# A new order of VectorE and ScalarE work between two layers, and block products of 384 + 384 columns

## The chip, the cores and the metric

The kernel runs on one core of a Trainium2 chip. The metric is the device time of one execution in microseconds. Three runs of the kernel before took 812.77 to 813.53 us, median 813.25. One more execution was taken by the profiler. PE is TensorE (PEld its weight loads), DVE is VectorE, ACT is ScalarE, POOL is GpSimd, SP issues most DMAs.

## The reference

```python
mask = q_assign[:, :, :, None] == k_assign[:, :, None, :]     # nearest of 16 centroids
scores = np.where(mask, scale * np.matmul(q, k.transpose(0, 1, 3, 2)), -1e9)
attn_out = softmax(scores) @ v            # 2 x 8 heads, 768 tokens, 64 channels
x = attn_out.transpose(0, 2, 1, 3).reshape(1536, 512)
h = x @ w_in                              # layer 1, 512 -> 2048
x = softplus(h) @ w_out                   # 2048 -> 512
g = x @ w_gate                            # layer 2, 512 -> 1536
y = (g * sigmoid(g) * (x @ w_val)) @ w_out2   # 1536 -> 512
```

The attention's inputs are float32, the weights float64 in this case, the result float32. Every matmul outside the transposes is made of three: each operand is split into a high part in the engine's rounded float32 form and the low remainder, and high x high, high x low and low x high are summed in PSUM.

## The kernel before

The attention fills the first 250 us or so; the change does not touch it. After it the 1536 tokens lie as columns of `XH` and `XL` (high and low part), with the 512 channels in four pieces of 128 rows.

**Layer 1** runs over 16 *units* of 128 hidden columns (`h_unit`). A unit multiplies the four channel pieces of its weight with all tokens into three PSUM banks of 512 columns (36 matmuls, `proj`). ACT then reads each bank twice (Abs into `e`, Relu into `r`), takes Exp and Ln of `e`, DVE adds `r` and `e`, ACT casts the sum to its high part `gh`, and DVE subtracts for the low part `gl`. Two units at a time go into `y_group(g)`, which multiplies with their `w_out` rows. It has four *blocks*, one for each 128 output channels, of three banks and 18 matmuls: nine for the first unit, nine for the second. DVE adds each bank to `acc`. There are eight banks, handed out in turn, so that a block's third bank can be the one that a unit or block some banks earlier still holds. On PE, units 14 and 15 stand before y_group 6 (units 12 and 13) and y_group 7 (units 14 and 15). In y_group 7 the finished `acc` is also split into `YH` (ACT) and `YL` (DVE and POOL), the input of layer 2.

**Weights** come as 512 KB loads (`raw`, three buffers). Each float64 weight is narrowed to float32: ACT takes the Abs of the upper words, DVE does two TENSOR_SCALAR and two SCALAR_TENSOR_TENSOR (`m`), then the split into `whi` (a cast, by DVE in layer 1, by ACT in layer 2) and `wlo` (DVE). This work is cut into three tasks per weight (`first`, `second`, `third`) in a deque `todo`; `pump` takes a few tasks from it after each piece of matmuls. So the order in which the program text calls tasks is the order of each engine's queue, and every engine works its queue strictly from the front.

**Layer 2** has 12 units. The first two are *plain*: gate and val products of 36 matmuls each (`plain_unit`), Silu of the gate banks on ACT into `sg`, product with the val banks on DVE. The other ten (`s_unit`) use a block scheme with seven products of half the inner size and half the tokens instead of eight. For it `t_sums` makes four differences of quarters of `acc` (in place, DVE) and splits each into `Th` (ACT) and `Tl` (DVE). One product (`prod`) has 2 x 3 weights and for each weight two matmuls, of 512 and of 256 columns, into a tile of 768 of two banks. The results go through tiles `x`, `w`, `y`, ACT copies and DVE additions. The second matrix `w_out2` is applied in `o_piece`, 12 matmuls for 256 tokens into a tile of two banks, one for each 128 tokens (a *token tile*); nine such pieces at the end are added to the earlier result by DVE, one addition per token tile, and stored.

The lines that matter: L858, L859 (`split_g`), L877 to L888 (`h_unit`), L908 to L930 (`y_group`), L1032 to L1045 (`t_sums`), L1072 and L1081 (`plain_unit`), L1096 (`o_piece`), L1124 (`prod`), L1156 (first copy of an `s_unit`), L1225 and L1229 (the last additions), L123 to L150 (narrowing and splitting a weight).

Of the kernel before, what the change touches and what calls it, by code (L numbers as in the profile page):

```python
# [11 lines left out]
F32 = mybir.dt.float32  # L12
# [3 lines left out]
AF = mybir.ActivationFunctionType  # L16
# [24 lines left out]
def kernel(  # L41
# [143 lines left out]
    def pair_of(f):  # L185
        return [(("gate", f), cols_of(w_gate, f), None), (("val", f), cols_of(w_val, f), None)]
# [4 lines left out]
    for f in range(NF2):  # L191
        stream += (pair_of(f + 1) if NPLAIN <= f + 1 < NF2 else []) + last_of(NF1 + f)
# [40 lines left out]


# [631 lines left out]
    def h_unit(f, banks=None):  # L866
        if banks is None:
            banks = [bank() for _ in range(NCH)]
            w = need(W, ("in", f))
            for half in range(2):  # L870
                proj(XH, XL, w, banks, range(2 * half, 2 * half + 2))
                pump()
        e = tp.tile([128, NTOK], F32, tag="e", name="e")
        r = tp.tile([128, NTOK], F32, tag="s", name="r")
        for c in range(NCH):
            cs = slice(512 * c, 512 * c + 512)
            nc.scalar.activation(out=e[:, cs], in_=banks[c], func=AF.Abs)  # L877
# [12 lines left out]
        def split_part():  # L890
            g_t[f] = split_g(e, "g")

        return [log_part, sum_part, split_part], split_tasks(batches.pop(0))

    def y_group(g):
# [3 lines left out]
        for d0 in range(0, KD, nd):  # L899
# [31 lines left out]
            if not last:  # L931
                pump()

# [4 lines left out]
    for g in range(NF1 // 2):  # L938
        if 2 * g + 2 < NF1:
            for f in (2 * g + 2, 2 * g + 3):  # L940
                soft, split = h_unit(f)
                if f < NF1 - 2:
                    todo.extend([soft[0]] + split[:3] + [soft[1]] + split[3:6] + [soft[2]] + split[6:])
                else:
                    first_do(soft + split[:3])
                    todo.extend(split[3:])
        else:
            YH = keep.tile([128, KD, NTOK], F32R, tag="xh", name="YH")
            YL = keep.tile([128, KD, NTOK], F32R, tag="xl", name="YL")
# [31 lines left out]
    S_t, T_t = {}, {}  # L981
# [47 lines left out]
    def t_sums():  # L1029

        q = [[acc[:, 2 * k:2 * k + 2, HT * t:HT * t + HT] for t in range(2)] for k in range(2)]
        nc.vector.tensor_tensor(out=q[0][0], in0=q[0][1], in1=q[0][0], op=ALU.subtract)  # L1032
        nc.vector.tensor_tensor(out=q[0][1], in0=q[1][1], in1=q[0][1], op=ALU.subtract)
        nc.vector.tensor_tensor(out=q[1][1], in0=q[1][1], in1=q[0][0], op=ALU.subtract)
        nc.vector.tensor_tensor(out=q[1][0], in0=q[1][0], in1=q[1][1], op=ALU.subtract)

# [10 lines left out]
        tasks = []  # L1047
        for n, x in ((3, q[0][1]), (2, q[1][1]), (4, q[1][0]), (1, q[0][0])):
            tasks += [functools.partial(high, n, x), functools.partial(low, n, x)]
        return tasks  # L1050

    def plain_unit(f):
        gb = [bank() for _ in range(NCH)]
        wg = need(W, ("gate", f))
        if f == 0:
            vb = [bank() for _ in range(NCH)]
            wv = need(W, ("val", f))
            proj(YH, YL, wg, gb, range(KD - 1))
            pump2(4)
            proj(YH, YL, wv, vb, range(KD - 1))  # L1060
            pump2(3)
            proj(YH, YL, wg, gb, range(KD - 1, KD))
            proj(YH, YL, wv, vb, range(KD - 1, KD))
            pump2(2)
# [50 lines left out]
    def s_unit(f):  # L1115
# [59 lines left out]
        y = psx.tile([128, 1024], F32, tag="Y", name="y")[:, 0:HT]  # L1175
# [11 lines left out]
        a_half(f, sg, 0)  # L1187
        a_half(f, sg, 1)
# [3 lines left out]
    todo.extend(split_tasks(last_of(NF1)))  # L1192
    todo.extend(plain_unit(0))
    todo.extend(pair_tasks(2))
    todo.extend(split_tasks(last_of(NF1 + 1)))
# [66 lines left out]
```

## Time and profile before

| what | us |
| --- | --- |
| median of three runs | 813.25 |
| the profiled execution | 813.9 |
| its span, first to last instruction | 812.1 |
| PE busy in the span | 791.0 |
| DVE busy | 654.5 |
| ACT busy | 500.8 |

The time of an execution is 1.8 us more than its span. Start times below count from the span's beginning. A matmul's row shows its start and a modelled duration that overlaps with the next one, so the pace of PE is read from the distance between starts. A bracket at a row's end says how long the engine sat idle before it and which instruction ended that.

### The profile page before, as it was taken

What the parts mean: (1) busy time and instruction counts of PE and PEld (TensorE: products, weight loads), DVE (VectorE), ACT (ScalarE), POOL (GpSimd) and SP (SyncE); (2) the same over time, 40 slices, a digit from 0 to 9 for tenths busy, and PEclk for the clock granted to TensorE, in tenths of its full rate; (3) what the DMA queues carried; (4) which work ended last, traced back from release to release, by engine and by line L of the source; (5) the groups of instructions that cost most, each with busy time, mean ns of one, the idle gap of its engine ahead of it and who ended that gap; (6) DMA issues with size and microseconds to landing.
All of it is one profiled execution on the core that took longest, in us unless ns stands there. A gap on an engine that the chain in (4) does not pass through costs nothing.

```text
span 812.1 us, 12093 instructions
## 1 busy us (share of the span) xinstructions
PE 791.0 (97%) x4485; PEld 689.6 (85%) x4485; DVE 654.5 (81%) x1047; ACT 500.8 (62%) x893; POOL 163.0 (20%) x160
## 2 busy tenths in 40 slices
PE   8999999999999999999999999989999999999997
PEld 7898999999998778888888887867888888888886
DVE  6988988888895997989879778889777777777763
ACT  5888889889895587365563744355544655555520
POOL 5736456555522000000000000400000101011100
PEclk9999999999999999999999999999999999999999
DMA  7875865675411322222121210012435676767454
GB/s 177 238 180 128 204 145 145 168 164 138 98 40 31 104 78 78 76 81 78 52 78 55 76 52 28 25 39 92 155 132 115 144 147 138 154 120 142 85 176 155
DMA packets 69339, 91.57 MB, mean 113 GB/s; under 512 B 29376, under 2 KB 52000, under 8 KB 69280
## 3 DMA queue, kind: packets, MB, share of 16 engines
q1 hardware_dynamic: 64688, 79.40, 34.6%
q0 software_dynamic: 3024, 11.01, 9.0%
q8 instruction: 35, 0.57, 0.3%
q10 hardware_dynamic: 1568, 0.39, 0.2%
q14 instruction: 24, 0.20, 0.1%
HBM read 51.41 MB, written 17.35 MB: 85 GB/s over the span
## 4 chain that ended last, share of the span: by engine, by line
PE 81%; DVE 12%; ACT 3%; DMA 2%; issue 1%; POOL 0%; DVEq 0%; ACTq 0%; SPq 0%; POOLq 0%
PE bank L908 14%; PE bank L818 13%; PE ob L1096 12%; PE x L1124 10%; PE ops L558 7%; PE tps L541 7%; PE sps L509 7%; PE w L1124 5%; PE y L1124 3%; PE mps L383 1%; PE sims L420 1%; DVE m L135 1%; DVE m L132 1%; DVE acc L922 1%; DVE wlo L150 1%
## 5 line engine op out<-in xcount | busy, mean ns | idle before, releaser
L548 DVE TENSOR_TENSOR tl<-tps,th 128x384 fp32r<-128x384 f32 x192 | 98.8, 550 | 14.8 <-ACT th L547 14.5
L517 DVE TENSOR_REDUCE nm<-sps 128x1 f32<-128x768 f32 x96 | 91.3, 952 | 14.1 <-PE sps L509 11.5
L547 ACT CAST th<-tps 128x384 fp32r<-128x384 f32 x192 | 84.6, 490 | 18.6 <-PE tps L541 16.0
L541 PE MATMUL tps<-id,p 128*128 128x128 f32 x576 | 93.1, 278 | 1.5 <-DVE tl L548 1.5
L525 ACT ACTIVATE p<-sps,nm 128x768 f32<-128x768 f32 x96 | 88.2, 919 | 1.6 <-DVE nm L517 1.6
L509 PE MATMUL sps<-KT,QT 128*128 128x384 f32 x384 | 83.4, 339 | 1.7 <-ACT p L525 1.7
L541 PEld LDWEIGHTS tps<-id,p 128*128 128x128 f32 x576 | 75.1, 151 | 8.1 <-DVE tl L548 4.2
L558 PE MATMUL ops<-th,VV 128*128 128x256 f32 x288 | 80.1, 307 | 0.0
L558 PE MATMUL ops<-tl,VV 128*128 128x256 f32 x288 | 72.7, 282 | 0.0
L858 ACT CAST gh<-e 128x1536 fp32r<-128x1536 f32 x16 | 23.8, 1487 | 73.0 <-DVE e L888 73.0
L509 PEld LDWEIGHTS sps<-KT,QT 128*128 128x128 f32 x384 | 63.3, 189 | 2.6 <-ACT p L525 2.4
L1113 POOL DMA_DIRECT2D out_dram<-side x21 | 18.2, 868 | 227.5 <-ACT side L1109 227.5
L150 DVE TENSOR_TENSOR wlo<-m,whi 128x512 fp32r<-128x512 f32 (+1 forms) x66 | 43.0, 651 | 24.2 <-ACT whi L149 22.5
L930 POOL TENSOR_TENSOR YL<-acc,YH 128x512 fp32r<-128x512 f32 x7 | 9.3, 1322 | 260.6 <-ACT YH L924 260.4
L922 DVE TENSOR_TENSOR acc<-bank,acc 128x512 f32<-128x512 f32 x84 | 53.0, 681 | 6.4 <-PE bank L908 6.4
L908 PE MATMUL bank<-gh,whi 128*128 128x512 f32 x192 | 54.5, 391 | 2.2 <-DVE whi L149 1.1
L1096 PE MATMUL ob<-whi,aa 128*128 128x512 f32 x168 | 56.5, 390 | 0.0
L558 PEld LDWEIGHTS ops<-tl,VV 128*128 128x128 f32 x288 | 54.7, 190 | 0.1
L818 PE MATMUL bank<-XH,whi 128*128 128x512 f32 x192 | 54.1, 390 | 0.7 <-DVE whi L149 0.7
L558 PEld LDWEIGHTS ops<-th,VV 128*128 128x128 f32 x288 | 54.4, 189 | 0.2
L908 PE MATMUL bank<-gl,whi 128*128 128x512 f32 x192 | 54.0, 389 | 0.0
L908 PE MATMUL bank<-gh,wlo 128*128 128x512 f32 x192 | 54.0, 389 | 0.0
(199 smaller groups left out, 1938.4 us busy)
## 6 DMA issues: line engine op xcount, KB each, us to landing
raw<-in_moe_w_out_dram SPq DMA_DIRECT2D x28, 512.0 KB, 3.3
out_dram<-side POOLq DMA_DIRECT2D x21, 512.0 KB, 5.6
raw<-in_moe_w_in_dram SPq DMA_DIRECT2D x16, 512.0 KB, 3.7
raw<-in_moe_w_val_dram SPq DMA_DIRECT2D x12, 512.0 KB, 4.4
raw<-in_moe_w_gate_dram SPq DMA_DIRECT2D x12, 512.0 KB, 3.4
QT<-hi SPq DMA_DIRECT2D x30, 192.0 KB, 3.0
KT<-hi SPq DMA_DIRECT2D x14, 384.0 KB, 5.6
kn<-in_k_dram SPq DMA_DIRECT2D x16, 192.0 KB, 3.9
```

The source lines that it names most:

```text
L509: nc.tensor.matmul(ps[:, c, 0:384], lhsT=Q[:, a, 128 * j:128 * j + 128], rhs=K[:, a, 384 * c:384 * c + 384], start=(a == 0), stop=(a == 1),)
L517: nc.vector.tensor_reduce(out=nm, in_=ps[:, :, 0:384], axis=AX.XY, op=ALU.max, negate=True)
L525: nc.scalar.activation(out=_h(p), in_=s_t.pop(i)[:, :, 0:384], func=AF.Exp, bias=nm_t.pop(i), accum_out=sm_t[pr][:, j:j + 1],)
L541: nc.tensor.transpose(ps[:, 128 * j:128 * j + 128], p[:, 128 * kb:128 * kb + 128], id32)
L547: nc.scalar.copy(th, pv)
L548: nc.vector.tensor_tensor(out=tl, in0=pv, in1=_r(th), op=ALU.subtract)
L558: nc.tensor.matmul(o[:, 0:CW], lhsT=VV_t[pr][:, hh, kb].rearrange("p a d -> p (a d)"), rhs=t[:, kb, :], start=(kb == 0 and lohi == 0), sto ...
L818: nc.tensor.matmul(banks[c], lhsT=wt[:, kk, :], rhs=xt[:, kk, 512 * c:512 * c + 512], start=(kk == 0 and wt is hi and xt is xh), stop=(kk ...
L908: nc.tensor.matmul(banks[NCH * d + c], lhsT=wt[:, 0, ds_], rhs=gt[:, 512 * c:512 * c + 512], start=(ff == 0 and n == 0), stop=(ff == 1 and ...
L922: nc.vector.tensor_tensor(out=a, in0=bk, in1=a, op=ALU.add)
L1096: nc.tensor.matmul(bk[:, t, :], lhsT=lhs[:, ts_], rhs=rhs[:, 0, :], start=(ff == 0 and i == 0), stop=(ff == 1 and i == 2),)
L1124: nc.tensor.matmul(dst[:, cs], lhsT=wt[:, at + kk, :], rhs=x(part, kk)[:, cs], start=(first and kk == 0 and wt is hi and part == 0), stop= ...
```

## The change

- Units 14 and 15: the weight rows 14 and the gate weight 1 are now narrowed between the steps of unit 14's softplus, and rows 15 inside y_group 6. `h_unit(15)` and the blocks of y_groups 6 and 7 take given numbers of tasks instead of what `pump` chooses.
- Both `w_out2` weights of the plain units are loaded earlier and narrowed in y_group 7 (`two_tasks`), with the cast on ACT; `high_on` is set before y_group 7.
- The first T difference is made inside y_group 7; the other three and three of the four `Th` casts follow in one task, the last `Th` comes after the first plain unit's Silu.
- A one-column Silu of the identity, with a one-column DVE copy behind it, stands ahead of the first real Silu, so that the table is loaded there.
- `prod` uses 384 + 384 columns, each half in a bank of its own; `sg`, `p1`, `x`, `w`, `y` are viewed accordingly.
- `o_piece` finishes one token tile before it begins the other.

```diff
+    def two_tasks(keys, tag):
+        m_t = {}
+        def first():
+            for key in keys:
+                while key not in loaded_t:
+                    load_ahead(len(loaded_t) + 1)
+                m_t[key] = w_narrow(loaded_t.pop(key))
+                next(m_t[key])
...
+        return [first, second, third] + [functools.partial(split, key) for key in keys]
...
                 proj(XH, XL, w, banks, range(2 * half, 2 * half + 2))
-                pump()
+                if f < NF1 - 1:
+                    pump()
+                else:
+                    for _ in range(4):
+                        todo.popleft()()
...
+    def t_sum(n):
+        nc.vector.tensor_tensor(
+            out=quad[(0, 0, 1, 1)[n]][(0, 1, 1, 0)[n]],
+            in0=quad[(0, 1, 1, 1)[n]][(1, 1, 1, 0)[n]],
+            in1=quad[(0, 0, 0, 1)[n]][(0, 1, 0, 1)[n]],
+            op=ALU.subtract,
+        )
...
-            if not last:
+            if g == NF1 // 2 - 2:
+                for _ in range((0, 2, 1, 9)[d0]):
+                    if todo:
+                        todo.popleft()()
+            elif not last:
                 pump()
+            elif d0 < 3:
+                for _ in range((2, 1, 2)[d0]):
+                    late.popleft()()
+                if d0 == 1:
+                    t_sum(0)
...
-                    first_do(soft + split[:3])
-                    todo.extend(split[3:])
+                    while todo and todo[0] in begun:
+                        todo.popleft()()
+                    todo.extendleft(reversed([soft[0]] + split[:3] + [soft[1]] + split[3:5] + [soft[2]] + split[5:]))
...
+            high_on.append(1)
+            while todo:
+                todo.popleft()()
+            late = collections.deque(two_tasks([("out2", f) for f in range(NPLAIN)], "b"))
         y_group(g)
...
+        def sums():
+            for n in range(1, 4):
+                t_sum(n)
+            for n, x in order[:3]:
+                high(n, x)
...
+        if f == 0:
+            nc.scalar.activation(out=sg[:, 0:1], in_=id32[:, 0:1], func=AF.Silu)
+            nc.vector.tensor_copy(sg[:, 0:1], id32[:, 0:1])
...
-        for ff in range(2):
-            hi, lo = need(W, ("out2", 2 * g + ff))
-            ah, al = (x[n // 3] for x in a_t[2 * g + ff])
-            for t in range(2):
+        for t in range(2):
+            for ff in range(2):
+                hi, lo = need(W, ("out2", 2 * g + ff))
+                ah, al = (x[n // 3] for x in a_t[2 * g + ff])
...
-                    for cs in CH:
+                    for c in range(2):
                         nc.tensor.matmul(
-                            dst[:, cs],
+                            dst[:, c, :],
                             lhsT=wt[:, at + kk, :],
-                            rhs=x(part, kk)[:, cs],
+                            rhs=x(part, kk)[:, HT // 2 * c:HT // 2 * c + HT // 2],
```

First place: ACT's queue after unit 14. `e_5695` and `gh_5745` or `gh_5761` belong to unit 14, `raw_5543` is weight rows 14, `raw_5667` rows 15, `raw_5609` gate weight 1, `bank_5703` to `bank_5705` the banks of unit 15. In the kernel before:

```order
L885 ACTIVATE e_5695<-e_5695 128x1536 [waits Activation_49]
L858 CAST gh_5745<-e_5695 128x1536 [waits DVE_49]
L123 ACTIVATE m_5749<-raw_5543 128x512 [waits DMAHW0_49]
L877 ACTIVATE e_5753<-bank_5703 128x512 [waits PE_49]
L881 ACTIVATE r_5754<-bank_5703 128x512
```

And in the changed kernel:

```order
L916 ACTIVATE e_5695<-e_5695 128x1536 [waits Activation_49]
L123 ACTIVATE m_5726<-raw_5543 128x512 [waits DMAHW0_49]
L123 ACTIVATE m_5757<-raw_5609 128x512 [waits DMAHW1_49,DVE_49]
L885 CAST gh_5761<-e_5695 128x1536 [waits DVE_49]
L908 ACTIVATE e_5765<-bank_5703 128x512 [waits PE_49]
```

The Abs of two weights now stand ahead of unit 14's cast; the reads of unit 15's banks stand behind that cast in both.

Second place: DVE's queue from unit 14's addition (`e_5695`) to the first `acc` additions of y_group 6. `m_5749` and `m_5726` are weight rows 14, `m_5757` gate weight 1, `m_5783` rows 15, `bank_5761` and `bank_5787` the first bank of y_group 6. In the kernel before:

```order
L888 TENSOR_TENSOR e_5695<-r_5696,e_5695 128x1536 [waits Activation_49]
L859 TENSOR_TENSOR gl_5746<-e_5695,gh_5745 128x1536 [waits Activation_49]
L125 TENSOR_SCALAR m_5749<-m_5749 128x512 [waits Activation_49]
L128 TENSOR_SCALAR m_5749<-m_5749 128x512 [waits DVE_49]
L922 TENSOR_TENSOR acc_4053<-bank_5761,acc_4053 128x512 [waits PE_49]
```

And in the changed kernel:

```order
L150 TENSOR_TENSOR wlo_5735<-m_5726,whi_5734 128x512 [waits DVE_49]
L919 TENSOR_TENSOR e_5695<-r_5696,e_5695 128x1536
L125 TENSOR_SCALAR m_5757<-m_5757 128x512 [waits Activation_49]
L128 TENSOR_SCALAR m_5757<-m_5757 128x512 [waits DVE_49]
L886 TENSOR_TENSOR gl_5762<-e_5695,gh_5761 128x1536 [waits Activation_49]
L132 SCALAR_TENSOR_TENSOR m_5757<-raw_5609,m_5757 128x512 [waits DMAHW1_49,DVE_49]
L135 SCALAR_TENSOR_TENSOR m_5757<-raw_5609,m_5757 128x512 [waits DVE_49]
L149 CAST whi_5777<-m_5757 128x512 [waits DVE_49,PE_49]
L150 TENSOR_TENSOR wlo_5778<-m_5757,whi_5777 128x512 [waits DVE_49,PE_49]
L125 TENSOR_SCALAR m_5783<-m_5783 128x512 [waits Activation_49]
L128 TENSOR_SCALAR m_5783<-m_5783 128x512 [waits DVE_49]
L965 TENSOR_TENSOR acc_4053<-bank_5787,acc_4053 128x512 [waits PE_49]
```

All of weight rows 14 now stands ahead of unit 14's addition, and the first `acc` addition of y_group 6 stands behind the first two instructions of weight rows 15, which wait for ACT.

Third place: DVE's queue up to the one-column copy, which writes the same `sg` as the Silus, and ACT's at the first Silu. DVE in the changed kernel:

```order
L931 TENSOR_TENSOR acc_4053<-acc_4053 128x2x768 [waits DVE_49]
L1097 TENSOR_TENSOR Tl_6055<-acc_4053,Th_6054 128x1536 [waits Activation_49]
L1097 TENSOR_TENSOR Tl_6058<-acc_4053,Th_6057 128x1536 [waits Activation_49]
L1097 TENSOR_TENSOR Tl_6061<-acc_4053,Th_6060 128x1536 [waits Activation_49]
L1131 COPY sg_6138<-id32_72 128x1 [waits Activation_49]
```

ACT in the kernel before (the four casts of `acc` to `Th` precede):

```order
L1041 CAST Th_6114<-acc_4053 128x1536 [waits PE_49,Activation_49]
L1072 ACT_TABLE_LOAD
L1072 ACTIVATE sg_6118<-bank_6016 128x512 [waits PE_49]
L1072 ACTIVATE sg_6118<-bank_6017 128x512 [waits PE_49]
L1072 ACTIVATE sg_6118<-bank_6018 128x512 [waits PE_49]
```

ACT in the changed kernel:

```order
L1093 CAST Th_6060<-acc_4053 128x1536 [waits DVE_49,PE_49]
L1130 ACT_TABLE_LOAD
L1130 ACTIVATE sg_6138<-id32_72 128x1
L1134 ACTIVATE sg_6138<-bank_6045 128x512 [waits DVE_49,PE_49]
L1134 ACTIVATE sg_6138<-bank_6046 128x512 [waits PE_49]
```

The table load moved ahead of a Silu that reads no bank; the first Silu that reads one now waits for DVE too, where it waited for PE alone.

## Rows read from the trace of the kernel before

**Rows 1.** The page, part 1: busy us, share of the span, instructions
```profile
PE 791.0 (97%) x4485; PEld 689.6 (85%) x4485; DVE 654.5 (81%) x1047; ACT 500.8 (62%) x893; POOL 163.0 (20%) x160
```
**Rows 2.** Timeline of PE between the layers: start, us, engine, line, operation, tiles, count, idle
```profile
487.08 0.84 PE L908 MATMUL bank<-gh,whi 128*128 128x512 f32 x3
...
506.72 0.47 PE L908 MATMUL bank<-gh,whi 128*128 128x512 f32 x1 [1.12 <-DVE whi L149]
...
541.56 0.50 PE L818 MATMUL bank<-YH,whi 128*128 128x512 f32 x1 [3.50 <-ACT sg L1072]
...
559.17 0.50 PE L1124 MATMUL x<-YH,whi 128*128 128x512 f32 x2
...
564.60 0.62 PE L1124 MATMUL x<-Th,whi 128*128 128x512 f32 x2 [1.03 <-ACT p L1156]
```
**Rows 3.** Busy time by stretch: us, PE, PEld, DVE, ACT, POOL, PEclk, DMA, GB/s
```profile
506.00:510.00 4.00, 3.28 (x14) 2.74 (x15) 3.90 (x9) 0.00 (x0) 0.00 (x0) 1.00 0.41 131
542.00:546.00 4.00, 4.00 (x13) 3.09 (x12) 3.90 (x8) 1.05 (x2) 0.00 (x0) 0.58 0.00 0
```
**Rows 4.** Timeline of ACT, units 14 and 15
```profile
483.11 1.49 ACT L885 ACTIVATE e<-e 128x1536 f32<-128x1536 f32 x1
486.43 1.48 ACT L858 CAST gh<-e 128x1536 fp32r<-128x1536 f32 x1 [1.82 <-DVE e L888]
487.81 0.67 ACT L123 ACTIVATE m<-raw 128x512 f32<-128x512 f32 x1
488.37 0.59 ACT L877 ACTIVATE e<-bank 128x512 f32<-128x512 f32 x1
...
491.23 1.53 ACT L884 ACTIVATE e<-e 128x1536 f32<-128x1536 f32 x1
```
**Rows 5.** Timeline of DVE: one weight's six instructions, and the next
```profile
475.66 0.42 DVE L125 TENSOR_SCALAR m<-m 128x512 f32<-128x512 f32 x1
...
476.57 0.69 DVE L132 SCALAR_TENSOR_TENSOR m<-raw,m 128x512 int32<-128x512 int32 x1
...
479.10 1.75 DVE L859 TENSOR_TENSOR gl<-e,gh 128x1536 fp32r<-128x1536 f32 x1
```
**Rows 6.** Timeline of DVE in y_group 7 and the first plain unit
```profile
507.22 1.88 DVE L922 TENSOR_TENSOR acc<-bank,acc 128x512 f32<-128x512 f32 x3
509.02 0.41 DVE L125 TENSOR_SCALAR m<-m 128x512 f32<-128x512 f32 x1
...
535.51 6.76 DVE L1045 TENSOR_TENSOR Tl<-acc,Th 128x1536 fp32r<-128x1536 f32 x4 [0.69 <-ACT Th L1041]
```
**Rows 7.** Timeline of ACT before the first Silu
```profile
533.47 0.62 ACT L149 CAST whi<-m 128x512 fp32r<-128x512 f32 x1 [9.27 <-DVE m L135]
534.00 5.60 ACT L1041 CAST Th<-acc 128x1536 fp32r<-128x1536 f32 x4
539.62 1.28 ACT L1072 ACT_TABLE_LOAD   x1
```
**Rows 8.** Timeline of PE: a group of 384 columns; three pairs of a product
```profile
61.29 0.86 PE L509 MATMUL sps<-KT,QT 128*128 128x384 f32 x4
61.99 0.82 PE L541 MATMUL tps<-id,p 128*128 128x128 f32 x6
...
640.67 0.50 PE L1124 MATMUL x<-Th,whi 128*128 128x512 f32 x2
...
641.73 0.51 PE L1124 MATMUL x<-Th,whi 128*128 128x512 f32 x2
```
**Rows 9.** Timeline of all engines at the end
```profile
805.89 0.39 PE L1096 MATMUL ob<-whi,al 128*128 128x512 f32 x1
...
806.57 0.39 PE L1096 MATMUL ob<-whi,al 128*128 128x512 f32 x1
806.99 0.69 DVE L1229 TENSOR_TENSOR part<-ob,part 128x512 f32<-128x512 f32 x1 [1.43 <-PE ob L1096]
```
**Rows 10.** The page, part 6: issues, KB each, median us to landing
```profile
raw<-in_moe_w_out_dram SPq DMA_DIRECT2D x28, 512.0 KB, 3.3
```

More of the change, by code (lines that the diff above doesn't have):

```diff
@@ L190 @@
     stream = [w for batch in batches for w in batch]
-    for f in range(NF2):
-        stream += (pair_of(f + 1) if NPLAIN <= f + 1 < NF2 else []) + last_of(NF1 + f)
+    stream += [w for f in range(NPLAIN) for w in last_of(NF1 + f)] + pair_of(NPLAIN)
+    for f in range(NPLAIN, NF2):
+        stream += (pair_of(f + 1) if f + 1 < NF2 else []) + last_of(NF1 + f)
     W = {}
@@ L232, in split_tasks, with second, third, split @@
         return tasks
+    def two_tasks(keys, tag):
[6 more added lines that the diff above has]
+                next(m_t[key])
+        def second():
+            for key in keys:
+                next(m_t[key])
+        def third():
+            for key in keys:
+                m_t[key] = next(m_t[key])
+            load_ahead(3)
+        def split(key):
+            pool, bufs = pool_of[tag]
+            W[key] = w_split(m_t[key], pool, tag, bufs)
+        return [first, second, third] + [functools.partial(split, key) for key in keys]
     todo = collections.deque()
@@ L893, in h_unit @@
         return [log_part, sum_part, split_part], split_tasks(batches.pop(0))
+    HT = NTOK // 2
+    quad = [[acc[:, 2 * k:2 * k + 2, HT * t:HT * t + HT] for t in range(2)] for k in range(2)]
+    T_t = {}
+    def t_sum(n):
[5 more added lines that the diff above has]
+        )
     def y_group(g):
@@ L944 @@
                 else:
-                    first_do(soft + split[:3])
-                    todo.extend(split[3:])
+                    while todo and todo[0] in begun:
+                        todo.popleft()()
+                    todo.extendleft(reversed([soft[0]] + split[:3] + [soft[1]] + split[3:5] + [soft[2]] + split[5:]))
+                    if f == NF1 - 1:
+                        todo.popleft()()
+                        for _ in range(2):
+                            todo.popleft()()
         else:
@@ L979, in pump2 @@
             todo.popleft()()
-    S_t, T_t = {}, {}
+    S_t = {}
     def pair_tasks(f):
@@ L1029, in t_sums @@
     def t_sums():
[L1031 to L1035, printed above, removed]
         def high(n, x):
@@ L1045, in low @@
             nc.vector.tensor_tensor(out=_h(tl), in0=x, in1=_r(_h(th)), op=ALU.subtract)
[L1047 to L1050, printed above, removed]
+        def sums():
[3 more added lines that the diff above has]
+                high(n, x)
+        order = ((3, quad[0][1]), (2, quad[1][1]), (4, quad[1][0]), (1, quad[0][0]))
+        return [sums] + [functools.partial(low, n, x) for n, x in order[:3]] + [
+            functools.partial(high, *order[3]), functools.partial(low, *order[3])
+        ]
     def plain_unit(f):
@@ L1057, in plain_unit @@
             wv = need(W, ("val", f))
+            for _ in range(2):
+                todo.popleft()()
             proj(YH, YL, wg, gb, range(KD - 1))
-            pump2(4)
+            for _ in range(2):
+                todo.popleft()()
             proj(YH, YL, wv, vb, range(KD - 1))
-            pump2(3)
             proj(YH, YL, wg, gb, range(KD - 1, KD))
             proj(YH, YL, wv, vb, range(KD - 1, KD))
-            pump2(2)
         else:
@@ L1174, in s_unit @@
         more()
-        y = psx.tile([128, 1024], F32, tag="Y", name="y")[:, 0:HT]
+        y = psx.tile([128, 2, 512], F32, tag="Y", name="y")[:, :, 0:HT // 2]
         prod(y, g1, 2, quarter(1, 0), True)
@@ L1186, in s_unit @@
         fill(2)
-        a_half(f, sg, 0)
-        a_half(f, sg, 1)
+        a_half(f, sg_all, 0)
+        a_half(f, sg_all, 1)
     side = [tp.tile([128, NTOK], F32, tag="s", name="side") for _ in range(2)]
     todo.extend(t_sums())
[L1192 to L1195, printed above, removed]
+    rest = plain_unit(0)
+    todo.extend(rest)
+    todo.extend(pair_tasks(NPLAIN))
     rest = plain_unit(1)
```

16 lines of the change are left out of this document (8 added, 8 removed).

## The prediction

> **What bounds the kernel now.** I read the page first: PE is busy 97% of the span [rows 1], so time is won only where PE stands still or where a matmul gets shorter. Then I went through PE's own timeline for the places at which it waits between the layers, asked the ACT and DVE timelines for what ended each wait, and the order of the changed program for who now stands in front of whom.
>
> Four losses lie there [rows 2, 3]. PE waits 1.12 us at 506.72 for the weight of unit 15 (`whi`, written by DVE). It waits 3.50 us at 541.56, where the third matmul of the second plain unit needs the bank that Silu reads. [...] Its price: from that matmul on 70 stand before the first block product, at 0.227 us each (three in 806.57 - 805.89 = 0.68 [rows 9]); 541.56 + 70 x 0.227 = 557.45, but the product starts at 559.17, 1.72 us late. The fourth loss is 1.03 us at 564.60, for an ACT copy. Together 1.12 + 3.50 + 1.72 + 1.03 = 7.4 us.
>
> Why the Silu is late: ACT idles 9.27 us until DVE has merged a weight, then casts four T sums (5.60 us), then loads the table (1.28 us) [rows 7]. The 1.72 us of low clock cost nothing in the end: the copy waited for at 564.60 stands behind DVE and ACT work, so at full clock that wait would have been 2.75 us.
>
> **Part 1, units 14 and 15.** Before, ACT finishes the logarithm of unit 14 at 483.11 + 1.49 = 484.60, DVE adds (ACT waits 1.82 us for it), ACT casts at 486.43, and from 488.37 it empties the three banks of unit 15 [rows 4, 5]. The change puts the whole weight 14 ahead of that addition: its Abs on ACT, then six DVE instructions, which take 479.10 - 475.66 = 3.44 us [rows 5]. So: Abs 484.6 to 485.25 (0.67), DVE six 488.7, addition 490.4 (1.75, as the 1536-column row at 479.10), cast 1.48 to 491.9, and only then the banks of unit 15. PE needs the first of them as third bank of the second block of y_group 6; y_group 6 starts at 487.08 [rows 2], a block is 18 x 0.227 = 4.08 us, so at 487.08 + 4.08 + 0.45 = 491.6. The emptying of one bank takes a third of 491.23 - 488.37 = 2.86 us [rows 4], so it is free at 492.9. **New wait: 1.3 us.**
>
> It goes on. The three banks end at 494.7, Exp and Ln of unit 15 take 3.05 us (1.53 + 1.49 and a step) to 497.7, the Abs of weight 15 ends at 498.3. On DVE the first two instructions of weight 15 stand ahead of the first `acc` addition, and they wait for that Abs: 0.91 us (475.66 to 476.57) to 499.2, the addition 0.68 to 499.9. PE needs that bank again as third bank of the third block: 487.08 + 2 x 4.08 + 1.3 + 0.45 = 497.0. **New wait: 2.9 us.** In return weight 15 is ready in time: the wait at 506.72 goes (the matmul was due nine after y_group 7's start, 503.4 + 2.04 = 505.44, so 1.28 by start times). y_group 7 starts at 487.08 + 16.3 + 4.2 = 507.6 instead of 503.4.
>
> **Part 2, VectorE between the layers.** From 499.2 DVE has one long queue until the little COPY that follows the early Silu. By the changed order it holds: 24 `acc` additions, three in 1.80 us (507.22 to 509.02) [rows 6], 14.4; the rest of weight 15, 479.10 - 476.57 = 2.5; addition and low part of unit 15, 2 x 1.7 = 3.4; two `out2` weights without their DVE cast, 2 x (3.44 - 0.45) less the overlap of interleaved instructions, 5.5; five `YL` of the `acc` size, 3.1; four T sums of 1536 columns at 1.75, 7.0; three `Tl` at 6.76 / 4, 5.1. That is 41.0 us. Four times DVE also waits for an ACT cast that in turn needs DVE's last addition (the `out2` Abs, the `out2` casts, the `YL`); the nearest row is the 0.69 us that DVE idles for one such cast at 535.51 [rows 6]; where a YH cast of 0.6 us stands before it, 1.3. Two of each make 4.0, of which the first starts a little early; I take 3.8 us; bounds 1.4 (two round trips) and 7.6 (twice what I take). So the COPY runs at 499.2 + 41.0 + 3.8 = 544.0, and the first real Silu, which waits for it since both write `sg`, frees its bank at 544.65.
>
> PE on its side: 507.6, + 16.3 for y_group 7, + 16.3 for the first plain unit, + about 1.0 (the low part of unit 15 arrives 0.2 late; the third matmul of the plain unit waits 0.8 for an `acc` addition that stands behind the first T sum), + 0.45: 541.65. **New wait 3.0 us**, at the same place as the old one. The table load lies ahead of it unseen, but so it buys nothing: what ended last on ACT is now DVE's queue.
>
> Balance up to the second plain unit: its third matmul runs at 544.65 instead of 541.56, +3.1. What follows: before it lost 1.72 and, by start times, 564.60 - 563.4 = 1.2. After, DVE has no `out2` weight left in front of the multiplications, so the copy is in time; 544.65 + 70 x 0.227 + 4.24 (two products; 559.17 to 563.4) = 564.8. So +0.2 if the clock stays up and all of the 564.60 wait goes (it comes back as 1.1 at most). If the clock falls once more after a 3.0 us wait, 1.7 is on top, with no later wait to hide it. The wait of 1.12 us was followed by a granted clock of 1.00 over 506 to 510, the 3.50 us one by 0.58 [rows 3]; 3.0 is nearer to 3.5: I take the fall. A fall already after the 2.9 us wait costs nothing more, since DVE's queue doesn't wait for PE there; it only shortens the 3.0. **Part 1 and 2: 0.2 + 1.7 = +1.9 us; bounds -2.1 (no fall, the Silu 2.4 us earlier and so nearly when PE is there: 0.2 - 2.3) and +5.7 (the Silu 3.8 later).**
>
> **Part 3, 384 + 384.** 7 products x 10 units x 6 = 420 pairs. Three pairs of 512 + 256 take 641.73 - 640.67 = 1.06, 353 ns a pair. Four matmuls of 384 columns take 61.99 - 61.29 = 0.70, 350 ns a pair [rows 8]. 420 x 3.5 ns = 1.5 us saved. Bounds: 768 columns at the pace of the 512 alone (0.68 / 3 x 1.5 = 340 ns [rows 9]), 5.6 us; on the other side 0.7 lost, if a group took 0.71. I take 1.5, from the same shape. [...]
>
> **Part 4, the last pieces.** The last matmul for one token tile now stands six instead of three from the end. But before, the last matmuls start at 805.89, 806.11, 806.34 and 806.57, and the addition of the first tile starts at 806.99, after the end of the very last [rows 9], though its own tile was done 0.68 us earlier. It waits for the whole bank pair, and the bank pair is still one tile. 0; the other end is one addition, -0.6.
>
> **Loads.** SP issues the two `out2` weights ahead of the next gate and val pair. A 512 KB load lands in 3.3 us [rows 10], and the pair is used over 20 us later: 0.
>
> **Sum.** The profiled execution has 813.9 us, 812.1 in its span; the median of the runs is 813.25 and I add to that: 813.25 + 0.2 + 1.7 - 1.5 = 813.65.
>
> **Rivals.**
> A, the clock stays up in the second plain unit. For it: 3.0 is under 3.5, and a fall in y_group 6 would shorten it to some 1.5. Against: it is far from 1.12. 813.25 + 0.2 - 1.5 = 811.95.
> B, the new waits don't come, because the bank or the COPY is in fact not waited for. Then the four losses go and no other comes: 813.25 - 7.4 - 1.5 = 804.35. Against it are the waits that the order names.
> C, slower: DVE's queue. If the casts that it waits for cost 7.6 instead of 3.8, every microsecond goes to the Silu and to the end, as nothing later absorbs it: 813.65 + 3.8 = 817.4. It decides from the point at which the COPY starts after 545.5.
> D, a pair costs by its 768 columns and two fixed parts, however split, so 384 + 384 gives nothing: 813.65 + 1.5 = 815.15. For it: the 353 and 350 ns lie close. Against it: 512 alone run at 227 ns, so 512 + 256 is dearer than its columns.
>
> **Chances.** Forecast 0.37, A 0.25, B 0.13, C 0.17, D 0.08. A measurement of this kernel tells some 0.2%, 1.6 us, from no change: 811.6 to 814.9 is the same. The forecast and half of A lie inside; the rest of A, B and the deep end of part 3 are faster, 0.27; C, D and some of the forecast's upper bound slower, 0.23; same 0.50. The range: 809.5 (A with 2.5 us more from part 3) to 816.5 (most of C). B lies outside. The likeliest case alone: 811.5 to 815.5.
>
> **What would show it.** Right: PE waits of about 1.3 and 2.9 us in y_group 6, none for `whi` in y_group 7, one near 3.0 us before the second plain unit with the DVE COPY just ahead of the Silu, a clock below 1.0 behind it, none in the first block unit, pairs of 350 ns, the last addition still behind the last matmul. Wrong: PE without waits in y_group 6, a Silu that starts when its bank is full, or pairs of 340 ns.

## The result, and the profile after

The changed kernel takes 820.03 us (median; 818.2 to 822.49), the kernel before 814.68 us in the same series: ratio 1.0065, 95% interval 1.0044 to 1.0087. It is slower, and the time lies above the predicted range of 809.5 to 816.5 us. The median of before was 813.25 us in the runs that the prediction started from, so 1.4 us of the 6.4 us between forecast and result are the base; the other 5 are to be explained.

The profiled execution has a span of 819.1 us (812.1 before). Its page, part 1, answers to [rows 1]:

```profile
PE 793.3 (97%) x4485; PEld 708.7 (87%) x4485; DVE 659.6 (81%) x1049; ACT 500.8 (61%) x893; POOL 163.9 (20%) x160
```

VectorE is busy for 5.1 us more, with two instructions more. That is a first hint. Where PE lost the time shows in its timeline between the layers (start, us, engine, line, operation, tiles, count, idle before and what ended it), which answers to [rows 2]:

```profile
489.33 0.84 PE L951 MATMUL bank<-gh,whi 128*128 128x512 f32 x3
...
495.16 0.50 PE L951 MATMUL bank<-gh,whi 128*128 128x512 f32 x1 [1.14 <-ACT r L912]
...
502.07 0.50 PE L951 MATMUL bank<-gh,whi 128*128 128x512 f32 x1 [2.51 <-DVE acc L965]
...
530.80 0.47 PE L845 MATMUL bank<-YH,whi 128*128 128x512 f32 x1 [2.35 <-DVE acc L965]
...
550.90 0.79 PE L845 MATMUL bank<-YH,whi 128*128 128x512 f32 x1 [3.50 <-ACT sg L1134]
...
568.41 0.51 PE L1186 MATMUL x<-YH,whi 128*128 128x384 f32 x2
...
572.60 0.51 PE L1186 MATMUL x<-Th,whi 128*128 128x384 f32 x2
```

Two waits in y_group 6, none for `whi` in y_group 7, one in the first and one in the second plain unit, none in the first block unit. The granted clock by stretch (columns as in [rows 3]) shows that it fell twice, after the second and after the fourth wait:

```profile
502.00:507.00 5.00, 4.93 (x15) 3.91 (x16) 4.90 (x10) 0.00 (x0) 0.00 (x0) 0.66 0.00 0
550.00:554.00 4.00, 3.10 (x7) 2.48 (x8) 2.83 (x6) 2.93 (x4) 0.00 (x0) 0.59 0.00 0
```

I cut the span at three starts of PE: y_group 6, the first block product, the last matmul. Every kernel below is read by this table (us, from one profiled execution each).

| kernel | start to y_group 6 | y_group 6 to first product | product to last matmul | after it |
|---|---|---|---|---|
| before | 487.08 | 72.09 | 247.39 | 5.56 |
| changed | 489.33 | **79.09** | 245.16 | 5.56 |
| e1_384 | 486.48 | 72.09 | 246.55 | 5.55 |
| e2_tokens | 487.60 | 73.39 | 246.08 | 5.57 |
| e3_no_copy | 493.53 | 74.45 | 246.36 | 5.56 |
| e4_units | 486.65 | 78.54 | 245.16 | 5.55 |
| e5_no_pool | 487.31 | 78.17 | 245.16 | 5.56 |
| e7_no_copy2 | 490.06 | 74.47 | 245.16 | 5.55 |
| e8_spare | 491.56 | 72.07 | 247.53 | 5.57 |
| e6d_order | 485.31 | **67.31** | 247.57 | 5.56 |
| e9_table | 490.47 | 67.30 | 247.57 | 5.57 |

The change costs 7.0 us between y_group 6 and the first product and gives 2.2 back behind it. The 2.25 us before y_group 6 lie in the attention, which the change doesn't touch: the first matmul of layer 1 starts at 256.61 us instead of 254.35, and from there to y_group 6 it is 232.72 us, before 232.73. The mean granted clock over the first 21 us is 0.84 in this execution and 0.92 before. One execution's value of that column says little: e6d_order and e9_table, whose code is the same up to y_group 6, differ by 5.2 us in it, with 1.00 and 0.92 over the first 21 us.

Why the stretch is longer: the Silu of the first plain unit waits for the one-column COPY on VectorE. ACT's timeline there, answering to [rows 7]:

```profile
546.68 1.28 ACT L1130 ACT_TABLE_LOAD   x1
547.98 0.20 ACT L1130 ACTIVATE sg<-id 128x1 f32<-128x1 f32 x1
550.25 1.57 ACT L1134 ACTIVATE sg<-bank 128x512 f32<-128x512 f32 x3 [2.07 <-DVE sg L1131]
```

The table is there at 547.96, and ACT then idles 2.07 us for a copy of one column. And VectorE comes to that copy late. Its timeline from the first `acc` addition behind the new wait:

```profile
501.33 3.67 DVE L965 TENSOR_TENSOR acc<-bank,acc 128x512 f32<-128x512 f32 x6
...
515.35 1.29 DVE L965 TENSOR_TENSOR acc<-bank,acc 128x512 f32<-128x512 f32 x2 [0.91 <-PE bank L951]
...
519.27 1.06 DVE L125 TENSOR_SCALAR m<-m 128x512 f32<-128x512 f32 x1 [1.26 <-ACT m L123]
...
520.71 0.42 DVE L125 TENSOR_SCALAR m<-m 128x512 f32<-128x512 f32 x1
...
523.48 0.68 DVE L965 TENSOR_TENSOR acc<-bank,acc 128x512 f32<-128x512 f32 x1
524.08 1.27 DVE L132 SCALAR_TENSOR_TENSOR m<-raw,m 128x512 int32<-128x512 int32 x1
525.39 1.67 DVE L135 SCALAR_TENSOR_TENSOR m<-raw,m 128x512 int32<-128x512 int32 x1
526.98 0.68 DVE L132 SCALAR_TENSOR_TENSOR m<-raw,m 128x512 int32<-128x512 int32 x1
527.69 0.69 DVE L135 SCALAR_TENSOR_TENSOR m<-raw,m 128x512 int32<-128x512 int32 x1
...
533.84 1.97 DVE L150 TENSOR_TENSOR wlo<-m,whi 128x512 fp32r<-128x512 f32 x2 [1.21 <-ACT whi L149]
...
550.02 0.14 DVE L1131 COPY sg<-id 128x1 f32<-128x1 f32 x1
```

The same instruction takes 1.06 us at 519.27 and 0.42 at 520.71, 1.27 at 524.08 and 0.68 at 526.98, 1.67 at 525.39 and 0.69 at 527.69. What runs beside the long ones stands in GpSimd's timeline:

```profile
517.37 2.67 POOL L973 TENSOR_TENSOR YL<-acc,YH 128x512 fp32r<-128x512 f32 x2 [260.73 <-ACT YH L967]
523.52 2.98 POOL L973 TENSOR_TENSOR YL<-acc,YH 128x512 fp32r<-128x512 f32 x2 [3.48 <-ACT YH L967]
531.99 2.67 POOL L973 TENSOR_TENSOR YL<-acc,YH 128x512 fp32r<-128x512 f32 x2 [5.48 <-ACT YH L967]
```

Each long one begins while GpSimd subtracts; that at 519.27 ends 0.3 us after GpSimd's pair (519.27 + 1.06 = 520.33; 517.37 + 2.67 = 520.04). The addition at 523.48, which reads a PSUM bank and `acc`, runs beside a subtraction too and takes its usual 0.68. Of the long ones, L132, L135 and L150 read two operands in SBUF, L125 reads one. What in a subtraction of GpSimd holds them up, no row shows; e5_no_pool below takes the subtractions away.

The end of the program, answering to [rows 9], has the first addition behind the very last matmul, as before:

```profile
813.57 0.39 PE L1158 MATMUL ob<-whi,al 128*128 128x512 f32 x1
814.00 1.29 DVE L1291 TENSOR_TENSOR part<-ob,part 128x512 f32<-128x512 f32 x2 [1.43 <-PE ob L1158]
```

### The profile page after: what moved, and what is told of

It is laid out like the page before. It is cut to its first block, busy times and chain, and to the rows that moved or that the text cites. A ratio compares the mean times of both kernels' runs of the same rounds, so it can differ in the third digit from the quotient of the medians.

```text
span 819.1 us, 12095 instructions
## 1 busy us (share of the span) xinstructions
PE 793.3 (97%) x4485; PEld 708.7 (87%) x4485; DVE 659.6 (81%) x1049; ACT 500.8 (61%) x893; POOL 163.9 (20%) x160
## 4 chain that ended last, share of the span: by engine, by line
PE 78%; DVE 11%; ACT 4%; DMA 4%; issue 1%; POOL 1%; SPq 0%; DVEq 0%; ACTq 0%; POOLq 0%
PE bank L845 14%; PE bank L951 13%; PE ob L1158 12%; PE x L1186 10%; PE ops L585 6%; PE tps L568 6%; PE sps L536 6%; PE w L1186 5%; PE y L1186 3%; DMA R<-rd 2%; DMA rd<-R 2%; PE mps L410 1%; PE sims L447 1%; DVE tl L575 1%; DVE nm L544 1%
## 5 line engine op out<-in xcount | busy, mean ns | idle before, releaser
L150 DVE TENSOR_TENSOR wlo<-m,whi 128x512 fp32r<-128x512 f32 (+1 forms) x66 | 43.5, 661 | 23.4 <-ACT whi L149 21.6
L1158 PE MATMUL ob<-whi,aa 128*128 128x512 f32 x168 | 59.6, 392 | 0.0
```

What stands on the lines that cost most here:

```text
L1158: nc.tensor.matmul(bk[:, t, :], lhsT=lhs[:, ts_], rhs=rhs[:, 0, :], start=(ff == 0 and i == 0), stop=(ff == 1 and i == 2),)
```

## The experiments

Ratios are to the kernel before, with 95% intervals.

**The split alone (e1_384).** The kernel before with

```
-  for cs in CH: matmul(dst[:, cs], rhs=x(part, kk)[:, cs])
+  for c in range(2): matmul(dst[:, c, :], rhs=x(part, kk)[:, HT//2*c:HT//2*c + HT//2])
```

> The kernel before with 384 + 384 columns alone. Measured in the trace from the first block product to the last matmul (before 806.57 - 559.17 = 247.40 us, changed kernel 813.57 - 568.41 = 245.16). Theory 1: the pairs run at 174 ns a matmul, 348 instead of 353 ns a pair, so 420 x 5 ns: 245.2 to 245.5 us, and the whole time 2 us shorter. Theory 2: the changed kernel's stretch is shorter only because the wait of 1.2 us in the first block unit is gone, and the split gives under 1 us: 246.5 or more.

Measured: 813.2 us, ratio 0.9986 (0.9976 to 0.9997). Product to last matmul is 0.84 us shorter (theory 2: under 1 us), the stages behind y_group 6 are otherwise as before. PE's timeline shows why it isn't the 1.5 predicted. In the changed kernel, a run of 18 pairs, then 12 fill matmuls of 512 columns, and the next product:

```profile
639.28 0.51 PE L1186 MATMUL w<-Th,whi 128*128 128x384 f32 x2
...
645.52 0.39 PE L1158 MATMUL ob<-whi,aa 128*128 128x512 f32 x1
...
648.28 0.51 PE L1186 MATMUL x<-Th,whi 128*128 128x384 f32 x2
```

and the same in the kernel before:

```profile
631.59 0.51 PE L1124 MATMUL w<-Th,whi 128*128 128x512 f32 x2
...
637.95 0.40 PE L1096 MATMUL ob<-whi,aa 128*128 128x512 f32 x1
...
640.67 0.50 PE L1124 MATMUL x<-Th,whi 128*128 128x512 f32 x2
```

18 pairs take 6.24 us instead of 6.36, but the fill takes 2.76 instead of 2.72, with the same 12 matmuls. By the starts of all matmuls between 590 and 785 us a matmul of a product goes from 176.3 to 174.2 ns, a fill matmul from 227.5 to 230.0, in e1_384 as in the changed kernel. With 840 of the one and 324 of the other: -1.8 + 0.8 = -1.0, near the 0.84 measured. Why the fill gets slower stays open. It is not bound to the 384 columns: in e8_spare below, which has 512 + 256 columns and one unused tile more, a matmul of a product takes 173.4 ns and a fill matmul 232.6, read in the same way. So a pace that differs by 1 or 2% between two programs is not by itself an effect of the split. What speaks for it here is that e1_384 has no tile more and none of another size.

**The token order alone (e2_tokens).** The kernel before with

```
-  for ff in range(2): ... for t in range(2):
+  for t in range(2): for ff in range(2):
```

> The kernel before with one token tile after the other in the pieces, alone. Theory 1: six matmuls in a row into one bank run at 230 ns in the fills instead of 227, as the changed kernel's trace has it: 30 fills x 12 x 2.6 ns = 0.9 us more from the first block product to the last matmul (248.3 instead of 247.4 us), and nothing gained at the end, where the first addition still starts after the very last matmul. Theory 2: the 230 ns come from the 384-column neighbours; then 247.4 us. Theory 3: the addition of the first token tile starts earlier: 0.6 us less after the last matmul.

Measured: 814.45 us, ratio 0.9995 (0.9984 to 1.0006): nothing. After the last matmul 5.57 us, before 5.56, so theory 3 is out. A fill matmul takes 227.4 ns, so the token order is not what slows it, and theory 1 is out. (1.3 us moved from one stage to the other: in this execution the clock stayed low for longer after the Silu wait, 0.71 over 546 to 550 against 0.99 before, and the wait for `p` was gone in return.)

**Without the copy (e3_no_copy, e7_no_copy2).** The changed kernel with the early Silu into a column that no one needs, in e3 a new small tile, in e7 an old one:

```
-  activation(out=sg[:, 0:1], in_=id32[:, 0:1], func=AF.Silu)
-  tensor_copy(sg[:, 0:1], id32[:, 0:1])
+  activation(out=ss[:, 0:1], in_=id32[:, 0:1], func=AF.Silu)
```

> The changed kernel; the one-column Silu writes a tile of its own, and the one-column DVE copy is gone, so that the first real Silu doesn't wait for DVE. Measured from the first matmul of y_group 6 to the first block product (before 559.17 - 487.08 = 72.09 us, changed kernel 568.41 - 489.33 = 79.08). Theory 1 (the copy behind DVE's queue is what the Silu waits for): the Silu starts when the table is there, some 2.1 us earlier, the wait before the second plain unit falls from 3.5 to about 1.4 us, no low clock follows: 79.1 - 2.1 - 1.5 = 75.5 us. Theory 2 (ACT's own chain of Th casts and the table sets it): no more than 0.5 us shorter.

> The changed kernel without the one-column copy on VectorE: the early Silu writes its column into the old small tile ss, which nothing reads any more, instead of into sg. No new tile, so no address moves (e3_no_copy had a new small tile). All arithmetic that reaches the output is kept. Theory 1 (Silu of the first plain unit waits for VectorE's queue only through the copy; the 4 to 7 us that e3_no_copy lost before y_group 6 came from the new tile): from y_group 6 to the first block product 74 to 75.5 us as in e3_no_copy, start to y_group 6 486 to 490 us, time 814 to 817 us, 3 to 6 us under the changed kernel. Theory 2 (the early part of e3_no_copy was long for another reason, such as the order of instructions): start to y_group 6 again 492 us or more and time 819 us or more. Theory 3 (the copy is not what holds the stretch): 78.5 us or more from y_group 6 to the first block product.

Measured: e3 819.79 us, ratio 1.0074 (1.0059 to 1.0089); e7 816.12 us, ratio 1.0012 (0.9997 to 1.0027). Both cut the stretch to 74.5 us, 4.6 less than the changed kernel. In e3 this was eaten by 4 us before y_group 6; e7, without a new tile, keeps it. ACT's timeline of e7 shows the Silu right behind the table load, with no wait:

```profile
546.45 1.28 ACT L1130 ACT_TABLE_LOAD   x1
547.74 0.20 ACT L1130 ACTIVATE ss<-id 128x1 f32<-128x1 f32 x1
547.85 1.56 ACT L1133 ACTIVATE sg<-bank 128x512 f32<-128x512 f32 x3
```

So the copy is what tied the Silu to VectorE's queue. Not all of the 4.6 us are its price. In both executions the clock also stayed up after the second wait in y_group 6, where it fell in the changed kernel's: behind it three matmuls take 0.69 to 0.70 us by their starts (e3 from 506.62, e7 from 503.15), in the changed kernel up to 1.29. In e7 VectorE then had no wait of 0.91 us for PE. PE's waits in e7, and its clock there:

```profile
502.81 0.50 PE L951 MATMUL bank<-gh,whi 128*128 128x512 f32 x1 [2.50 <-DVE acc L965]
530.56 0.47 PE L845 MATMUL bank<-YH,whi 128*128 128x512 f32 x1 [2.77 <-DVE acc L965]
502.00:507.00 5.00, 4.19 (x18) 3.49 (x19) 4.96 (x9) 0.00 (x0) 0.00 (x0) 1.00 0.01 3
```

By the medians the copy costs 3.9 us (820.03 - 816.12, with the kernel before at 814.68 and 814.69), over half of the 7.0. The 2.4 us that e7 is above the stretch of before are its waits in y_group 6 and in the first plain unit and a low clock after the latter (0.72 over 530 to 536).

**The old order of units 14 and 15 (e4_units).** The changed kernel with the three blocks that pop tasks in unit 15, in y_group 6 and behind unit 14 put back as before.

> The changed kernel with the tasks of units 14 and 15 and of y_group 6 in the order of the kernel before. Same stretch as e3. Theory 1 (DVE's queue up to the Silu bounds the stretch): the waits of 1.1 and 2.5 us in y_group 6 and the low clock after them go, but the time comes back as longer waits in y_group 7 and before the plain units: 78 to 79.5 us. Theory 2 (those waits are the loss): 79.1 - 3.9 - 1.6 = 73.6 us.

Measured: 818.49 us, ratio 1.0061 (1.0037 to 1.0084), stretch 78.54. PE's waits there:

```profile
506.30 0.93 PE L947 MATMUL bank<-gh,whi 128*128 128x512 f32 x3 [1.12 <-DVE whi L149]
519.11 0.50 PE L947 MATMUL bank<-gh,whi 128*128 128x512 f32 x1 [1.78 <-DVE acc L961]
527.65 0.47 PE L845 MATMUL bank<-YH,whi 128*128 128x512 f32 x1 [2.54 <-DVE acc L961]
547.77 0.80 PE L845 MATMUL bank<-YH,whi 128*128 128x512 f32 x1 [3.54 <-ACT sg L1121]
```

The two waits of y_group 6 go and two others come, as theory 1 said: with the same work in VectorE's queue, the order of units 14 and 15 mainly chooses where PE waits for it (0.55 us of the 7.0 go).

**No subtraction on GpSimd (e5_no_pool).** The changed kernel with

```
-  eng = nc.gpsimd if c == 1 or c == 2 and d < KD - 1 else nc.vector
+  eng = nc.vector
```

> The changed kernel with all subtractions that make YL in y_group 7 on VectorE (the changed kernel gives seven of them to GpSimd). All arithmetic is kept. Read from the trace: VectorE's instructions on the out2 weights in y_group 7 (0.42 us by L125 and L132 and 0.69 us by L135 where GpSimd is idle; 1.06, 1.27 and 1.67 us beside GpSimd's subtractions in the changed kernel) and the stretch from y_group 6 to the first block product (79.09 us in the changed kernel). Theory 1 (VectorE is held up while GpSimd's subtractions run): the stretched instructions are back at 0.42 and 0.69 us and no cast takes over 1.4 us; VectorE gains 2.9 us and takes on about 4.3 us of subtractions, so the stretch is 79.5 to 81.5 us. Theory 2 (they are stretched for another reason, such as the weights' DMA): they stay at 1.0 us and more, and the stretch is 82.5 to 84 us. If VectorE's queue did not bound the stretch at all, it would stay at 79.1 or get shorter.

Measured: 817.94 us, ratio 1.0031 (1.0016 to 1.0047), stretch 78.17. VectorE's timeline, at the same instructions:

```profile
517.31 0.43 DVE L125 TENSOR_SCALAR m<-m 128x512 f32<-128x512 f32 x1 [0.65 <-ACT m L123]
...
522.51 0.69 DVE L132 SCALAR_TENSOR_TENSOR m<-raw,m 128x512 int32<-128x512 int32 x1
523.23 0.69 DVE L135 SCALAR_TENSOR_TENSOR m<-raw,m 128x512 int32<-128x512 int32 x1
...
531.13 1.29 DVE L150 TENSOR_TENSOR wlo<-m,whi 128x512 fp32r<-128x512 f32 x2 [0.61 <-ACT whi L149]
...
546.98 0.15 DVE L1131 COPY sg<-id 128x1 f32<-128x1 f32 x1
```

The stretched ones are back at 0.43, 0.69 and 1.29, so GpSimd's subtractions are what stretched them. My figure for the stretch was too high. What the expectation named as the sign of a queue that doesn't bound the stretch (79.1 us or less) came true, but that sign took for granted that the queue would get longer, and it got shorter: VectorE took over seven subtractions of 0.6 us, yet the COPY comes 59.67 us after y_group 6 instead of 60.69. Besides the 2.9 us of stretching it lost 1.9 us of waits for ACT (1.26 to 0.65, 1.21 to 0.61, and the last `YH` cast's 0.69 to none); the remaining 0.4 is spread over shorter steps. The stretch shrank with the queue, by 0.9 us, with the clock falling at the same two places as in the changed kernel (three matmuls take 1.28 us by their starts from 501.99 and from 549.80, otherwise 0.68). In this order GpSimd's help was worth less than nothing.

**An unused tile (e8_spare).** The kernel before with one more line, and no instruction more:

```
   sml.tile([128, 16], F32, name="fill2", bufs=1)
+  sml.tile([128, 16], F32, name="spare", bufs=1)
```

> The kernel before with one unused tile of 128 by 16 numbers more in the pool of small tiles, right behind fill2: no instruction is added, only the addresses of the small tiles of the attention move by 64 bytes a partition. All arithmetic is kept. Theory 1 (addresses of small tiles change the time of the attention, which is what e3_no_copy paid): start to y_group 6 longer than the 487.1 us of before by 2 us or more, time 816 to 821 us. Theory 2 (addresses are free): start to y_group 6 486 to 489.5 us and the time that of the kernel before within 0.3 per cent.

Measured: 818.2 us, ratio 1.0033 (1.0018 to 1.0047); start to y_group 6 491.56. So one unused tile makes the program 2.7 us slower by the ratio, and e3 against e7 points the same way. Where the loss lies is shown in part. From the first matmul of layer 1 to y_group 6, with the same 1020 matmuls, e8 takes 233.66 us and e3 233.65; every kernel without the new tile takes 232.72 to 232.74. The rest lies in the attention. The first 21 us of before and of e8 (stretch, busy us of PE, PEld, DVE, ACT, POOL, granted clock, DMA) show part of it:

```profile
0.00:21.00 21.00, 17.22 (x97) 15.29 (x97) 13.15 (x35) 12.74 (x24) 11.80 (x34) 0.92 0.78 183
```

```profile
0.00:21.00 21.00, 17.63 (x87) 15.70 (x88) 10.93 (x32) 10.86 (x20) 11.78 (x34) 0.84 0.75 178
```

In e8 the clock is lower on average and fewer instructions are done. But the changed kernel's profiled execution has 0.84 there too, with its small tiles where they were, and in e9_table, without the new tile, layer 1 begins at 257.75 us, in e8 at 257.90. So the single executions don't show that the attention is slower for the addresses. What the addresses do is not settled; that this tile is not free is.

**Another order between the layers (e6d_order).** The kernel before with the split into 384 + 384 and another order between the layers, told in words:

```
+  unit 15: Exp, Abs of its weight's first part, Ln, ... one by one (first_do)
+  while todo: todo.popleft()()              # ahead of t_sums
-  order of Th and Tl: 3, 2, 4, 1
+  order of Th and Tl: 1, 3, 2, 4
-  todo.extend(split_tasks(last_of(NF1 + 1)))  # between the layers
+  if f == NPLAIN: the same, in the first block unit
```

> A version that may beat both: the kernel before with the split into 384 + 384 columns, none of the changed kernel's reordering, and these moves: unit 15 makes the Abs of its next weight behind its Exp and Ln one by one; everything still in the queue of tasks is done before the four differences of acc; Th and Tl of quarter 1 first; the split of the second out2 weight moves from between the layers into the first block unit. All arithmetic is kept. Theory 1 (the stretch between the layers is bounded by the order of VectorE's and ScalarE's queues, and the waits of before, 1.12 for whi, 3.50 for Silu's tile and 1.03 for p, shrink when what they wait for is issued earlier): from y_group 6 to the first block product 68 to 70.5 us instead of 72.09, no low clock between the layers, and time 808 to 811 us. Theory 2 (each wait removed comes back elsewhere, as in e4_units): 71.5 to 73 us, time 812.5 to 814.5 us. Theory 3 (the moved split stretches the first block unit): product to last matmul 247.5 us or more instead of 246.55.

Measured: 810.91 us, ratio 0.9941 (0.9921 to 0.9961), faster than both; stretch 67.31, less than theory 1 said, and no low clock in it (1.00 over 485 to 553). PE's waits between the layers are down to two:

```profile
535.77 0.50 PE L818 MATMUL bank<-YH,whi 128*128 128x512 f32 x1 [0.89 <-ACT sg L1075]
...
552.62 0.62 PE L1127 MATMUL x<-YH,whi 128*128 128x384 f32 x2 [0.69 <-ACT whi L149]
```

Theory 3 is right as well, but small: product to last matmul is 247.57 instead of 246.55.

**The early table load alone (e9_table).** e6d_order and one line ahead of the T sums:

```
+  nc.scalar.activation(out=ss[:, 0:1], in_=id32[:, 0:1], func=AF.Silu)
```

> e6d_order with one more instruction: a Silu of one column into the old small tile ss ahead of the four differences of acc, so that ScalarE loads Silu's table in idle time (the changed kernel's early table load alone, without its copy on VectorE). All arithmetic that reaches the output is kept. In e6d_order the load of 1.28 us stands at 533.83 right before the first Silu, and TensorE waits 1.04 us for that Silu and 0.84 us for whi and side before the first block product. Theory 1 (the load is on the path): the wait of 1.04 goes, nothing comes in its place, y_group 6 to the first block product 66.0 to 66.6 us instead of 67.31, time about 1 us under e6d_order. Theory 2 (VectorE's queue bounds the stretch whatever ScalarE does): the 1.04 goes, but the wait before the first block product grows from 0.84 to about 1.5 to 1.9, and the stretch stays at 67.1 to 67.4. Theory 3 (the early load itself hinders ScalarE's casts of whi and Th): 67.6 us or more.

Measured: 810.84 us, ratio 0.9939 (0.9918 to 0.9959), stretch 67.30. The load moves into idle time of ACT, PE's wait for the Silu goes, and the next one grows from 0.69 to 1.86:

```profile
528.90 1.28 ACT L1197 ACT_TABLE_LOAD   x1
```

```profile
557.77 0.61 PE L1127 MATMUL x<-YH,whi 128*128 128x384 f32 x2 [1.86 <-ACT whi L149]
```

Theory 2, to a tenth. The casts of `whi` that end the stretch wait for a `side` of VectorE, in e6d_order and in e9_table:

```profile
550.91 1.14 ACT L149 CAST whi<-side 128x512 fp32r<-128x512 f32 x2 [1.93 <-DVE side L1018]
```

```profile
556.06 1.14 ACT L149 CAST whi<-side 128x512 fp32r<-128x512 f32 x2 [1.93 <-DVE side L1018]
```

They start 65.60 and 65.59 us after y_group 6. So VectorE's queue sets the end of the stretch, and in this order the load is not on the path. (After the wait of 1.86 us the clock fell in e9, to 0.72 over 557 to 563; product to last matmul is 247.57 as in e6d, since two later waits of e6d, 0.69 at 574.09 and 0.62 at 582.00, went to none and 0.26.)

## Why the prediction was wrong

**Bounds now.** Right in the four losses: e6d_order brings the stretch down by 4.8 us and gives 1.0 back behind it. But they were read as four waits, each to be removed by itself. In the changed kernel (e4_units) and in e6d_order (e9_table) removing a wait brought another, with VectorE's queue behind both; for the kernel before itself that is argued and not run. The 1.72 us among the four are the price of the low clock behind the wait of 3.50 us: 0.50 over 542.8 to 546, where three matmuls take 1.28 us by their starts (543.80 to 545.08), and 0.68 from 546.25 on.

**Part 1.** Right: waits of 1.3 and 2.9 us predicted, 1.29 and 2.67 measured by start times (the rows have 1.14 and 2.51 idle), and the wait for `whi` gone. Wrong in one sentence: "A fall already after the 2.9 us wait costs nothing more, since DVE's queue doesn't wait for PE there". The clock fell (0.66 over 502 to 507), and VectorE idled 0.91 us for PE at 515.35. In e5_no_pool the clock fell there as well and VectorE waited 0.95 us; in e7_no_copy2 it stayed up at this place (1.00 over 502 to 507), and VectorE's five additions from 513.31 follow each other without a wait.

**Part 2, the step that failed.** The mechanism was right: the Silu waits for the COPY, the COPY for the whole queue, and the clock falls once more (0.59 over 550 to 554). The step that failed is the size of VectorE's queue. Predicted from the first `acc` addition to the COPY: 41.0 + 3.8 = 44.8 us. Measured 550.02 - 501.33 = 48.69, 3.9 us more: 2.9 of VectorE standing beside GpSimd's subtractions (0.64 + 0.59 + 0.98 + 0.68 from the rows above), 0.9 waiting for PE, 3.16 instead of 3.8 waiting for ACT, and the remaining 0.7 in short steps between instructions (VectorE is busy for 43.9 us of the 48.69; less the 2.9 that is the 41.0 forecast, so the count of instructions was right). PE's own side was late as well: the first plain unit waited 2.5 us instead of 0.8, and 1.6 of low clock lay in y_group 6 (16 matmuls from 502.07 on take 5.37 us; in e7_no_copy2, from 502.81, 3.77); so the wait at the second plain unit is 3.66 by start times, near the 3.0 predicted, but by luck: both sides of it moved by over 3 us. Against the predicted +1.9 stand 79.09 - 72.09 - 1.26 (the wait for `p`, gone as predicted) = +5.7. That is the upper bound that the prediction gave for parts 1 and 2; its range of time, up to 816.5, was cut off short of it.

The size is that of rival C, which was given 0.17, but not its cause: the casts that VectorE waits for cost less than forecast. I had taken each VectorE duration from rows in which GpSimd was idle, and the change moves just these instructions beside GpSimd. The clue stood in the trace of before, where one `YL` of VectorE took 0.96 us instead of 0.69, and began while GpSimd still subtracted (511.82 + 2.69 = 514.51):

```profile
514.10 0.96 DVE L930 TENSOR_TENSOR YL<-acc,YH 128x512 fp32r<-128x512 f32 x1
```

```profile
511.82 2.69 POOL L930 TENSOR_TENSOR YL<-acc,YH 128x512 fp32r<-128x512 f32 x2 [257.44 <-ACT YH L924]
```

**Part 3.** Right in sign, -0.8 instead of -1.5: the pairs gained slightly more than the 3.5 ns forecast (4.1), and the fill matmuls, which I had left out, lost half of it. Rival D (nothing) lies outside the interval of e1_384, narrowly.

**Part 4 and the loads.** Right, both 0: 5.56 us after the last matmul, as before, and no wait of PE between the layers ends with a load.

**Rivals A and B.** A is out, as the clock fell after the wait of 3.50 us before the second plain unit (0.59). B is out, as the new waits of 1.14 and 2.51 us came.

The sum again, with measured terms on the profiled spans: 812.1 + 5.7 - 1.0 (part 3, as this kernel has it) + 2.25 (before y_group 6) = 819.1. On the medians, 814.68 + 5.7 - 1.0 = 819.4; the other 0.6 us to 820.03 have no cause shown and lie within the interval.

## What to carry to other kernels

When work is moved, price it beside its new neighbours: here three of VectorE's instructions with two SBUF operands, and one TENSOR_SCALAR, took 0.59 to 0.98 us longer while GpSimd ran. Look at what a helper instruction is tied to: a copy of 0.14 us cost about 4 us, since it hung ScalarE on the longest queue. And where several waits have one queue behind them, take work out of that queue or put it later; removing a single wait (e4_units, e9_table) moved it to the next place.

## What the runs showed of the hardware

- VectorE beside GpSimd in the changed kernel: four instructions 0.59 to 0.98 us longer, an addition that reads PSUM not at all (0.68 us); the four back to their usual length without GpSimd's subtractions (e5_no_pool).
- A tile of 64 bytes a partition that nothing uses made the program 0.33% slower (e8_spare). In both kernels that have it, the 1020 matmuls from the start of layer 1 to y_group 6 took 0.93 us longer than in the nine others; the cause is open.
- Fill matmuls of the same shape took 227.5 ns before, 230.0 in e1_384 and 232.6 in e8_spare; the cause is open.
- A wait alone did not settle the clock: after 2.51 us idle it fell in the changed kernel (0.66 over 502 to 507), after 2.50 at the same place in e7_no_copy2 it stayed up (1.00 over the same stretch). It also fell after shorter ones, of 1.78 us in e4_units (0.66 over 519 to 524) and of 1.86 in e9_table.
